# Listing the evictions of out in block order in a fused attention and FFN kernel, with the work of every engine listed anew

## The chip, the cores and the metric

The kernel runs on one core of one Trainium2 chip. The metric is the device time of one execution in microseconds (us); the time of the kernel before is the median of 3 runs. Engines are called as in the profile: PE is TensorE's matrix unit and PEld its weight loads, DVE is VectorE, ACT is ScalarE, POOL is GpSimd, SP is SyncE, which here only issues DMAs.

## The reference

```python
# batch 8, heads 8, seq 576, head_dim 64; d_model 512, d_ff 1024, 4608 tokens
def _attn_ref(q, k, v):
    q_s = np.exp(q - q.max(-1, keepdims=True))
    q_s = q_s / (q_s.sum(-1, keepdims=True) + 1e-09)
    k_s = np.exp(k - k.max(2, keepdims=True))
    k_s = k_s / (k_s.sum(2, keepdims=True) + 1e-09)
    kv = np.einsum('bhsd,bhse->bhde', k_s, v)
    return np.einsum('bhsd,bhde->bhse', q_s, kv)

def _moe_ref(x, w1, w2, w3, w_out):
    a = x @ w1
    b = x @ w2
    h = a * b @ w3
    return h @ w_out
```

The output of the attention, with its heads side by side, is x of 4608 tokens by 512, and the output of the FFN is the result. All inputs and the output are float32.

## The kernel before

**Fold.** Since nothing stands between w3 and w_out, their product W3O = w3 @ w_out (1024 x 512) is made once at the start. w3 is loaded in six parts (`w3.0` to `w3.5`), w_out in two (`wo.0`, `wo.1`); for each of 8 row blocks ft, `w3t.ft` transposes on PE (L444), `w3T.ft` copies the transposed block out of PSUM, `pf.ft.0` and `pf.ft.1` multiply it with the two halves of w_out (L456), and `W3O.ft` evicts the product. Zero matmuls (L351, 17 at the very start and some ahead of one named step) fill time in which PE has nothing to do; the table `FILL` says ahead of which.

**Attention**, for each batch b. Steps are named for what they do, with b and, for most, the part of the tile: `q`, `k`, `v` load; `qmx` (L581) takes the maxima of q, `qsub` (L586) subtracts them, `qexp` is the exponential, `qsm`, `qeps`, `qrc` sum it and take the reciprocal, `qn` (L618) divides. The quotient is transposed on PE (`qt`, evicted by `qT`) or by a transposing DMA on SP's queue (`qd`, L641). `kmx`, `cba`, `cbx`, `cb` (L488 to L519) find the maxima of k, `ksub` (L523) subtracts, `kexp` (L531) is the exponential, `vc` casts v to float16. `kv` (L548, 72 small matmuls, then a few for the sum of k's exponentials) multiplies k and v, `kve` and `kv2` divide. `xm` (L666) and `xt` multiply with q and give x transposed, evicted by `xs` and `xts`.

**FFN**, for each token chunk c. Chunks 0 to 7 hold 512 tokens of batch c each, chunk 8 the remaining 64 tokens of all batches. For each of eight blocks u of d_ff: `up.1.c.sub.u` multiplies with w2 into a PSUM buffer of the ring pab, `bs.c.sub.u` evicts it as float16 to bsb (on ACT or DVE, L324), `up.0.c.sub.u` multiplies with w1 into another buffer of pab (both L783), and `ab.c.sub.u` (DVE, L798) multiplies the two. Then for each block of 128 tokens tb, `down.c.tb` multiplies with W3O into one of the two buffers of po (L805; L820 in chunk 8), `os.c.tb` evicts it to osb (ACT or DVE, L324) and `st.c.tb` stores it. The rings have 4 buffers in pab, 2 in po, 4 in osb, 4 in bsb. Chunks 0 and 1 are cut in two by `sub`, so that they can start before all of x is there.

**The order** is written out by hand: `ORDER` lists all 793 steps, and `Plan.run` (L48) emits them in that order, so each engine executes its own steps in the order of the list. For the flexible steps `PICKS` names the engine. Up to place `LINKED` of the list, steps of DVE and POOL that share a port are also tied to each other in list order. `Plan.run` checks that what a step needs is listed ahead of it, its `after` too; `after` makes no wait on the chip, it only says what has to be listed earlier. The buffers of a ring are those of the tile pool: which one a step gets, and whose release it waits for on the chip, follows from the order in which the list emits takes and releases. Loads listed in `LOADS` are issued on POOL's queue, with at most eight under way; those of `LATE` on SP's, where the stores and the transposing DMAs are too.

The places in the old list that matter below:

```
q.1.0 v.0 w3T.4 pf.5.1 ... kv.0 kve.0 ... qsub.1.0 w3t.1 pf.6.0 w3T.1 kv2.0
down.3.0 down.3.1 bs.4.0.1 qd.5.1 qd.5.0 os.3.1 os.3.0 v.7 down.3.2
```

Of the kernel before, what the change touches and what calls it, by code (L numbers as in the profile page):

```python
# [77 lines left out]
q.0.0 qmx.0.0 q.0.1 qmx.0.1 qsub.0.1 qexp.0.1 w3.4 wo.0 ident wo.1 qsub.0.0 w3.0 k.0 w3.2 w3.3 w3.5  # L78
w3t.4 w3t.5 w3T.5 pf.5.0 qsm.0.1 q.1.0 v.0 w3T.4 pf.5.1 qexp.0.0 qeps.0.1 qrc.0.1 qsm.0.0 w3.1 w3t.0
k.1 qn.0.1 qeps.0.0 pf.4.0 qrc.0.0 pf.4.1 qt.0.16 W3O.5 qn.0.0 w3T.0 qT.0.16 W3O.4 qt.0.8 pf.0.0  # L80
qt.0.0 w3t.2 w3T.2 w2.0 pf.0.1 w3t.3 w3T.3 kmx.0.0 cba.0 W3O.0 qT.0.8 cbx.0 pf.2.0 qT.0.0 pf.2.1
w1.0 w1.1 pf.3.0 w3t.7 w2.1 W3O.2 w3T.7 pf.3.1 w3t.6 pf.7.0 pf.7.1 w1.2 cb.0 ksub.0.1 kexp.0.1
ksub.0.0 kexp.0.0 kv.0 kve.0 w2.2 w3T.6 W3O.3 qmx.1.0 W3O.7 k.2 qsub.1.0 w3t.1 pf.6.0 w3T.1 kv2.0
xm.0.0 xs.0.0.0 xs.0.0.1 pf.1.0 pf.1.1 w2.3 xm.0.1 kmx.1.0 cba.1 pf.6.1 xs.0.1.1 xs.0.1.0 qexp.1.0
w1.3 v.1 q.1.1 q.2 cbx.1 qsm.1.0 up.1.0.0.0 xt.0 bs.0.0.0 up.0.0.0.0 up.1.0.1.0 up.0.0.1.0 ab.0.0.0
cb.1 qeps.1.0 ksub.1.1 ksub.1.0 bs.0.1.0 up.1.0.0.1 bs.0.0.1 ab.0.1.0 up.0.0.0.1 up.1.0.1.1
up.0.0.1.1 ab.0.0.1 bs.0.1.1 up.1.0.0.2 up.0.0.0.2 up.1.0.1.2 ab.0.1.1 up.0.0.1.2 W3O.1 kexp.1.1
qrc.1.0 xts.0.0 bs.0.0.2 up.1.0.0.3 ab.0.0.2 bs.0.1.2 kmx.2.0 kexp.1.0 cba.2 qn.1.0 bs.0.0.3 W3O.6
xts.0.1 up.0.0.0.3 up.1.0.1.3 ab.0.0.3 down.0.0 ab.0.1.2 cbx.2 cb.2 ksub.2.0 bs.0.1.3 kv.1
up.0.0.1.3 qmx.1.1 ksub.2.1 ab.0.1.3 kve.1 os.0.0 qsub.1.1 kv2.1 down.0.1 down.0.2 qd.1.0 kexp.2.0  # L90
kexp.2.1 os.0.1 qmx.2.1 xm.1.0 xs.1.0.1 xs.1.0.0 qmx.2.0 qsub.2.1 down.0.3 qexp.1.1 os.0.2
up.1.1.0.0 qsm.1.1 up.0.1.0.0 up.1.1.0.1 qexp.2.1 qeps.1.1 bs.1.0.0 qsm.2.1 qrc.1.1 qsub.2.0 v.2
vc.2.0 vc.2.1 ab.1.0.0 qexp.2.0 qsm.2.0 qn.1.1 qeps.2.1 bs.1.0.1 up.0.1.0.1 up.1.1.0.2 ab.1.0.1
qrc.2.1 st.0.0 k.3 q.3 kv.2 bs.1.0.2 qeps.2.0 kve.2 up.0.1.0.2 up.1.1.0.3 up.0.1.0.3 os.0.3 kv2.2
qt.1.16 qt.1.8 bs.1.0.3 ab.1.0.2 ab.1.0.3 qrc.2.0 down.1.0 qn.2.1 qT.1.8 qT.1.16 xm.1.1 xs.1.1.0
st.0.1 st.0.2 v.3 down.1.1 qn.2.0 qmx.3.0 qmx.3.1 qsub.3.0 qd.2.1 qd.2.0 kmx.3.0 xs.1.1.1 xt.1
up.1.1.1.0 up.0.1.1.0 xts.1.0 qexp.3.0 xts.1.1 os.1.1 bs.1.1.0 up.1.1.1.1 up.0.1.1.1 ab.1.1.0
bs.1.1.1 xm.2.0 cba.3 up.1.1.1.2 up.0.1.1.2 ab.1.1.1 qsm.3.0 xs.2.0.1 xs.2.0.0 xm.2.1 bs.1.1.2
up.1.1.1.3 up.0.1.1.3 cbx.3 xs.2.1.1 xs.2.1.0 up.1.2.0.0 ab.1.1.2 qsub.3.1 up.0.2.0.0 cb.3 bs.1.1.3
qeps.3.0 qrc.3.0 ab.1.1.3 st.0.3 k.4 qexp.3.1 bs.2.0.0 up.1.2.0.1 up.0.2.0.1 up.1.2.0.2 q.4 v.4 q.5  # L100
os.1.0 ksub.3.1 ksub.3.0 qsm.3.1 down.1.2 down.1.3 vc.3.1 qeps.3.1 vc.3.0 kmx.4.1 qrc.3.1 ab.2.0.0
kmx.4.0 cba.4 kexp.3.1 kexp.3.0 bs.2.0.1 up.0.2.0.2 os.1.3 ab.2.0.1 bs.2.0.2 qn.3.0 qmx.4.1 qn.3.1
ab.2.0.2 os.1.2 cbx.4 cb.4 up.1.2.0.3 kv.3 kve.3 kv2.3 bs.2.0.3 up.0.2.0.3 ab.2.0.3 up.1.2.0.4
up.0.2.0.4 xt.2 qd.3.0 qd.3.1 xts.2.1 up.1.2.0.5 up.0.2.0.5 xts.2.0 vc.4.0 qsub.4.1 bs.2.0.4 qmx.4.0
ab.2.0.4 bs.2.0.5 ab.2.0.5 xm.3.1 xm.3.0 xs.3.1.0 up.1.2.0.6 up.0.2.0.6 up.1.2.0.7 xs.3.0.1 xs.3.0.0
bs.2.0.6 xs.3.1.1 qmx.5.1 ksub.4.0 qsub.4.0 vc.4.1 ab.2.0.6 qexp.4.1 qexp.4.0 up.0.2.0.7 up.1.3.0.0
bs.2.0.7 up.0.3.0.0 up.1.3.0.1 qsm.4.1 ab.2.0.7 qeps.4.1 qsm.4.0 qrc.4.1 qsub.5.1 up.0.3.0.1
ksub.4.1 bs.3.0.0 qn.4.1 kexp.4.0 qeps.4.0 up.1.3.0.2 bs.3.0.1 down.2.0 qexp.5.1 kexp.4.1 ab.3.0.0
st.1.1 qrc.4.0 k.5 st.1.2 kmx.5.1 qmx.5.0 st.1.0 v.5 vc.5.0 st.1.3 q.6 ab.3.0.1 up.0.3.0.2 down.2.1
os.2.0 qd.4.1 qn.4.0 qd.4.0 kv.4 xt.3 bs.3.0.2 qsub.5.0 kmx.5.0 kve.4 os.2.1 cba.5 ab.3.0.2 down.2.2  # L110
down.2.3 vc.5.1 qexp.5.0 os.2.2 up.1.3.0.3 xts.3.1 os.2.3 xts.3.0 kv2.4 xm.4.0 qsm.5.1 bs.3.0.3
qeps.5.1 xm.4.1 xt.4 qsm.5.0 up.0.3.0.3 cbx.5 cb.5 qeps.5.0 xts.4.1 xts.4.0 qmx.6.0 ab.3.0.3
xs.4.0.0 xs.4.0.1 xs.4.1.1 xs.4.1.0 k.6 qrc.5.0 up.1.3.0.4 bs.3.0.4 up.0.3.0.4 up.1.3.0.5 up.0.3.0.5
ab.3.0.4 up.1.3.0.6 up.0.3.0.6 bs.3.0.5 ab.3.0.5 bs.3.0.6 up.1.3.0.7 up.0.3.0.7 up.1.4.0.0 qrc.5.1
ksub.5.1 ksub.5.0 q.7 st.2.2 kmx.6.1 kexp.5.1 kexp.5.0 ab.3.0.6 kv.5 up.0.4.0.0 st.2.1 qsub.6.0
qmx.7.0 qn.5.1 qn.5.0 bs.3.0.7 ab.3.0.7 bs.4.0.0 up.1.4.0.1 kve.5 ab.4.0.0 kmx.6.0 st.2.3 st.2.0 v.6
up.0.4.0.1 down.3.0 down.3.1 bs.4.0.1 qd.5.1 qd.5.0 os.3.1 os.3.0 v.7 down.3.2 qmx.6.1 kv2.5 cba.6
ab.4.0.1 up.1.4.0.2 os.3.2 xm.5.0 xm.5.1 xt.5 bs.4.0.2 cbx.6 qexp.6.0 xts.5.0 xts.5.1 up.0.4.0.2
up.1.4.0.3 up.0.4.0.3 up.1.4.0.4 qsub.7.0 qsub.6.1 vc.6.1 vc.6.0 qmx.7.1 xs.5.0.0 bs.4.0.3 xs.5.1.1
qexp.6.1 ab.4.0.2 qsm.6.0 ab.4.0.3 cb.6 bs.4.0.4 xs.5.1.0 up.0.4.0.4 ab.4.0.4 xs.5.0.1 up.1.4.0.5  # L120
up.0.4.0.5 bs.4.0.5 ab.4.0.5 up.1.4.0.6 up.0.4.0.6 bs.4.0.6 ab.4.0.6 up.1.4.0.7 up.0.4.0.7 bs.4.0.7
up.1.5.0.0 up.0.5.0.0 ksub.6.1 qeps.6.0 kexp.6.1 down.3.3 qsub.7.1 ab.4.0.7 up.1.5.0.1 up.0.5.0.1
ksub.6.0 vc.7.0 kexp.6.0 qexp.7.0 bs.5.0.0 qsm.6.1 qeps.6.1 qrc.6.0 qn.6.0 ab.5.0.0 qrc.6.1 qexp.7.1
bs.5.0.1 st.3.0 k.7 st.3.1 qn.6.1 vc.7.1 qsm.7.0 os.3.3 qsm.7.1 up.1.5.0.2 kv.6 up.0.5.0.2 kve.6
bs.5.0.2 down.4.0 down.4.1 os.4.0 qeps.7.0 down.4.2 up.1.5.0.3 ab.5.0.1 kv2.6 qd.6.0 qd.6.1 st.3.2
xm.6.0 ab.5.0.2 kmx.7.1 os.4.1 os.4.2 xm.6.1 xt.6 bs.5.0.3 st.3.3 qeps.7.1 qrc.7.1 qn.7.1 qd.7.1
st.4.0 up.0.5.0.3 xts.6.0 xts.6.1 ab.5.0.3 xs.6.0.0 xs.6.1.1 xs.6.0.1 kmx.7.0 up.1.5.0.4 up.0.5.0.4
up.1.5.0.5 bs.5.0.4 ab.5.0.4 bs.5.0.5 up.0.5.0.5 up.1.5.0.6 up.0.5.0.6 up.1.5.0.7 cba.7 ab.5.0.5
up.0.5.0.7 xs.6.1.0 cbx.7 bs.5.0.6 cb.7 ksub.7.1 ab.5.0.6 bs.5.0.7 ab.5.0.7 up.1.6.0.0 up.0.6.0.0
down.4.3 bs.6.0.0 ab.6.0.0 up.1.6.0.1 up.0.6.0.1 bs.6.0.1 ab.6.0.1 up.1.6.0.2 up.0.6.0.2 bs.6.0.2  # L130
up.1.6.0.3 up.0.6.0.3 ab.6.0.2 up.1.6.0.4 up.0.6.0.4 os.4.3 down.5.0 bs.6.0.3 up.1.6.0.5 ksub.7.0
qrc.7.0 qn.7.0 kexp.7.0 kexp.7.1 kv.7 ab.6.0.3 os.5.0 kve.7 st.4.1 st.4.2 qd.7.0 st.4.3 bs.6.0.4
ab.6.0.4 down.5.1 down.5.2 os.5.1 bs.6.0.5 kv2.7 os.5.2 up.0.6.0.5 xm.7.0 xm.7.1 xt.7 ab.6.0.5
xs.7.1.0 xts.7.1 xts.7.0 up.1.6.0.6 up.0.6.0.6 xs.7.1.1 bs.6.0.6 xs.7.0.0 xs.7.0.1 ab.6.0.6
up.1.6.0.7 up.0.6.0.7 up.1.7.0.0 up.0.7.0.0 bs.6.0.7 up.1.7.0.1 ab.6.0.7 down.5.3 bs.7.0.1 bs.7.0.0
ab.7.0.0 up.0.7.0.1 up.1.7.0.2 up.0.7.0.2 up.1.7.0.3 ab.7.0.1 up.0.7.0.3 bs.7.0.3 bs.7.0.2 ab.7.0.2
up.1.7.0.4 ab.7.0.3 up.0.7.0.4 up.1.7.0.5 up.0.7.0.5 bs.7.0.4 ab.7.0.4 bs.7.0.5 up.1.7.0.6
up.0.7.0.6 up.1.7.0.7 ab.7.0.5 up.0.7.0.7 bs.7.0.6 bs.7.0.7 ab.7.0.6 up.1.8.0.0 up.0.8.0.0 down.6.0
st.5.0 os.5.3 ab.7.0.7 os.6.0 down.6.1 down.6.2 st.5.1 os.6.1 down.6.3 bs.8.0.0 up.1.8.0.1 ab.8.0.0
up.0.8.0.1 up.1.8.0.2 bs.8.0.1 ab.8.0.1 st.5.2 os.6.2 down.7.0 up.0.8.0.2 up.1.8.0.3 up.0.8.0.3  # L140
st.5.3 st.6.2 bs.8.0.2 ab.8.0.2 os.7.0 st.6.0 st.6.1 os.6.3 down.7.1 os.7.1 st.7.1 st.7.0 bs.8.0.3
st.6.3 ab.8.0.3 up.1.8.0.4 bs.8.0.4 down.7.2 os.7.2 up.0.8.0.4 down.7.3 ab.8.0.4 os.7.3 up.1.8.0.5
bs.8.0.5 up.0.8.0.5 ab.8.0.5 up.1.8.0.6 up.0.8.0.6 bs.8.0.6 ab.8.0.6 up.1.8.0.7 bs.8.0.7 st.7.2
up.0.8.0.7 ab.8.0.7 down.8.0 down.8.1 os.8.0 down.8.2 os.8.1 down.8.3.0 os.8.2 down.8.3 st.7.3
st.8.0 st.8.1 st.8.2 os.8.3.0 st.8.3.0 os.8.3 st.8.3
# [778 lines left out]
```

## Time and profile before

| what | value |
|---|---|
| time, median of 3 runs | 240.86 us (240.09 to 241.2) |
| profiled execution, its own time | 240.74 us |
| span of the profiled execution | 239.0 us |
| PE busy | 229.9 us, 96% of the span |
| DVE busy | 179.8 us, 75% |
| ACT busy | 118.0 us, 49% |
| POOL busy | 111.4 us, 47% |

The profile is of one execution. Its span runs from the first to the last instruction that it shows; the execution's own time is 1.7 us longer. A row of the timeline has start, length, engine, line, operation, output and inputs with their shapes, and in brackets how long the engine had been idle before it and what ended that. A row of the waits has the engine and what it waited for, then the sum, the number of times and the longest.

### The profile page before, as it was taken

Reading aid. Unit: us, or ns where it says so; the run is one execution under the profiler, and the core shown is the slowest. Engines: PE = TensorE matmul, PEld = TensorE weight load, DVE = VectorE, ACT = ScalarE, POOL = GpSimd, SP = SyncE. Lnnn points to the kernel's source line nnn. Section 1 sums busy time; section 2 is a strip of 40 time slices with the busy share of each in tenths; the row PEclk is TensorE's granted clock in tenths of the full one; section 3 lists DMA queues with packets and bytes.
Section 4 is the critical chain, followed back from the end, with each engine's and each line's share of the span. In section 5 each row is a group of like instructions: output and inputs, shape, how many; then the busy total and the mean of one; then the engine's idle time right before and its main releaser. Section 6 shows DMA issues by size and latency. Waiting matters only on the chain.

```text
span 239.0 us, 4936 instructions
## 1 busy us (share of the span) xinstructions
PE 229.9 (96%) x1971; PEld 120.1 (50%) x1971; DVE 179.8 (75%) x273; ACT 118.0 (49%) x222; POOL 111.4 (47%) x74
## 2 busy tenths in 40 slices
...
GB/s 210 217 304 252 295 210 300 245 270 329 393 290 295 397 225 231 381 278 263 346 234 235 310 3 44 145 48 139 0 134 88 4 0 0 44 134 21 199 44 132
DMA packets 38998, 45.93 MB, mean 192 GB/s; under 512 B 17088, under 2 KB 23488, under 8 KB 38976
## 3 DMA queue, kind: packets, MB, share of 16 engines
...
q8 instruction: 15, 0.25, 0.4%
q14 instruction: 7, 0.06, 0.1%
...
## 4 chain that ended last, share of the span: by engine, by line
PE 76%; DMA 13%; POOL 4%; DVE 3%; ACT 1%; issue 1%; POOLq 0%; ACTq 0%
PE pab L783 47%; PE po L805 21%; DMA v<-in_v_dram 7%; DMA wosb<-in_moe_w_out_dram 4%; PE po L820 3%; DMA qT<-en 3%; POOL k L523 2%; PE pkv L548 2%; PE xm L666 1%; DVE kmx L497 1%; POOL q L586 1%; POOL en L618 1%; DVE kmx L498 1%; PE po L666 1%; ACT osb L324 0%
## 5 line engine op out<-in xcount | busy, mean ns | idle before, releaser
L798 DVE TENSOR_TENSOR ab<-pab,bsb 128x512 f16<-128x512 f32 x72 | 48.9, 682 | 25.9 <-PE pab L783 14.5
L783 PE MATMUL pab<-x,w1sb 128*128 128x512 f16 (+1 forms) x320 | 66.0, 337 | 0.0
L783 PE MATMUL pab<-x,w2sb 128*128 128x512 f16 (+1 forms) x320 | 65.9, 337 | 0.0
L805 PE MATMUL po<-W3O,ab 128*128 128x512 f16 x256 | 58.9, 379 | 0.7 <-ACT osb L324 0.7
L783 PEld LDWEIGHTS <-w2sb 128*128 128x128 f16 x352 | 34.0, 98 | 28.3 <-issue 0.9
L783 PEld LDWEIGHTS <-w1sb 128*128 128x128 f16 x352 | 33.7, 98 | 26.7
L324 ACT CAST bsb<-pab 128x512 f16<-128x512 f32 x46 | 26.8, 585 | 35.0 <-PE pab L783 29.0
L523 POOL TENSOR_TENSOR k<-k,cb 128x1152 f32<-128x1152 f32 x13 | 34.0, 2629 | 19.2 <-DVE cb L519 17.0
L805 PEld LDWEIGHTS <-ab 128*128 128x128 f16 x256 | 24.7, 98 | 29.9 <-issue 1.4
L324 ACT COPY osb<-po 128x512 f32<-128x512 f32 (+1 forms) x28 | 16.0, 571 | 41.6 <-PE po L805 31.9
L618 POOL TENSOR_TENSOR en<-eq,qr 128x1280 f16<-128x1280 f16 (+1 forms) x12 | 25.8, 2165 | 12.8 <-DMA out_dram<-osb 6.1
L586 POOL TENSOR_TENSOR q<-q,qm 128x1280 f32<-128x1280 f32 (+1 forms) x13 | 27.8, 2149 | 6.5 <-DMA qT<-en 4.5
L581 DVE TENSOR_REDUCE qm<-q 128x16 f32<-128x1024 f32 (+1 forms) x16 | 21.4, 1341 | 3.7 <-DMA q<-in_q_dram 3.7
L324 DVE CAST bsb<-pab 128x512 f16<-128x512 f32 x26 | 17.7, 685 | 6.2 <-PE pab L783 5.9
L599 DVE TENSOR_REDUCE qr<-eq 128x20 f32<-128x1280 f16 (+1 forms) x16 | 21.4, 1340 | 1.0 <-ACT eq L594 0.7
L531 ACT ACTIVATE ek<-k 128x1152 f16<-128x1152 f32 x16 | 18.3, 1161 | 5.3 <-POOL k L523 4.9
L594 ACT ACTIVATE eq<-q 128x1280 f16<-128x1280 f32 (+1 forms) x16 | 18.3, 1160 | 2.1 <-DVE q L586 1.7
L488 DVE TENSOR_REDUCE km<-k 128x128 f32<-128x1152 f32 x8 | 17.1, 2132 | 0.0
L456 PE MATMUL po<-wosb,w3T 128*128 128x512 f16 x64 | 15.6, 379 | 1.4 <-DMA wosb<-in_moe_w_out_dram 1.3
L324 DVE COPY osb<-po 128x512 f32<-128x512 f32 x9 | 6.2, 687 | 7.4 <-PE po L805 7.4
L328 ACT ACTIVATE x<-xm 128x512 f16<-128x512 f32 x16 | 9.1, 596 | 4.6 <-PE xm L666 4.5
L456 PEld LDWEIGHTS <-w3T 128*128 128x128 f16 x64 | 5.7, 98 | 7.6 <-issue 1.8
...
## 6 DMA issues: line engine op xcount, KB each, us to landing
...
```

The costliest lines, as they stand in the source:

```text
L324: return [(nc.scalar.copy if eng == "ACT" else engine[eng].tensor_copy)(out=out, in_=in_)]
L456: nc.tensor.matmul(st["pf", ft], lhsT=st["w3T", ft][:, gt, :], rhs=wosb[:, gt, :], start=(gt == 0), stop=(gt == N_FT - 1))
L523: return [engine[eng].tensor_tensor(out=kb[:, two(hp), :, :], in0=kb[:, two(hp), :, :], in1=st["cb", b][:, two(hp), None, :].broadcast_to( ...
L531: nc.scalar.activation(out=st["ek", b][:, hp, :, :].rearrange("p j (i d) -> p i j d", i=2), in_=kb[:, two(hp), :, :], func=AF.Exp)
L581: dve.tensor_reduce(out=st["qm", b][:, :, j], in_=qb[:, :, j, :], axis=AX.X, op=ALU.max)
L586: return [engine[eng].tensor_tensor(out=qb[:, :, j, :], in0=qb[:, :, j, :], in1=st["qm", b][:, :, j, None].broadcast_to([P, HH, n, D]), op ...
L594: nc.scalar.activation(out=st["eq", b, p], in_=qb[:, :, j, :], func=AF.Exp)
L599: dve.tensor_reduce(out=st["qr", b][:, :, slice(*PARTS[p])], in_=st["eq", b, p], axis=AX.X, op=ALU.add)
L618: return [engine[eng].tensor_tensor(out=st["en", b][:, j, :, :].rearrange("p j h d -> p h j d"), in0=st["eq", b, p], in1=st["qr", b][:, :, ...
L783: nc.tensor.matmul(st["p", one, c, sub, u][:, a * (t1 - t0):(a + 1) * (t1 - t0)], lhsT=w[:, ct, fb * P:(fb + 1) * P], rhs=x()[:, ct, t0:t1 ...
L798: dve.tensor_tensor(out=st["ab", c][:, nf * u:nf * u + nf, t0:t1], in0=cut(st["p", 0, c, sub, u]), in1=cut(st["bsb", c, sub, u]), op=ALU.mult)
L805: nc.tensor.matmul(st["po", c, tb], lhsT=st["ab", c][:, ft, tb * P:(tb + 1) * P], rhs=W3O[:, ft, :], start=(ft == 0), stop=(ft == N_FT - 1))
```

## The change

Each `os` step gets the previous one of its chunk (for the first, the last of the chunk before) in its `after`, so that the evictions of out have to be listed strictly in the order of their blocks. `ORDER`, `PICKS`, `LOADS` and `LATE` are written anew under that rule. The six zero matmuls stand ahead of `pf.4.0` instead of `pf.5.0`. The steps are the same 793, and what PE computes is the same.

```diff
 FILL = {
-    "begin": 17, "pf.5.0": 6,
+    "begin": 17, "pf.4.0": 6,
 }
...
+        old_os = [("os", c - 1, 3)] if c else []
...
                     A(("os", c, tb), moves(C), 0, lambda eng, tb=tb: os(tb, eng), [("down", c, tb)],
-                      lead=EVICT, gives=[("down", c, tb)], takes="osb")
+                      lead=EVICT, gives=[("down", c, tb)], takes="osb", after=old_os)
+                    old_os = [("os", c, tb)]
...
-                      lead=EVICT, gives=[("down", *it)], takes="osb")
+                      lead=EVICT, gives=[("down", *it)], takes="osb", after=old_os)
+                    old_os = [("os", *it)]
```

The loads:

```diff
 LOADS = [
-    ("w3", 4), ("wo", 0), ("wo", 1), ("w3", 0), ("k", 0), ("w3", 2), ("w3", 3), ("w3", 5), ("q",
-    1, 0), ("v", 0), ("w3", 1), ("k", 1), ("w2", 0), ("w1", 0), ("w1", 1), ("w2", 1), ("w1", 2),
-    ("w2", 2), ("k", 2), ("w2", 3), ("w1", 3), ("v", 1), ("q", 1, 1),
+    ("w3", 4), ("wo", 0), ("w3", 0), ("wo", 1), ("k", 0), ("w3", 2), ("w3", 3), ("w3", 5),
+    ("w3", 1), ("v", 0), ("q", 1, 0), ("k", 1), ("w2", 0), ("w1", 0), ("w2", 1), ("w1", 1),
+    ("w1", 2), ("w2", 2), ("k", 2), ("w2", 3), ("w1", 3), ("v", 1), ("q", 1, 1),
 ]
...
 LATE = [
-    ("q", 2), ("v", 2), ("k", 3), ("q", 3), ("v", 3), ("k", 4), ("q", 4), ("v", 4), ("q", 5),
-    ("k", 5), ("v", 5), ("q", 6), ("k", 6), ("q", 7), ("v", 6), ("v", 7), ("k", 7),
+    ("q", 2), ("v", 2), ("k", 3), ("q", 3), ("v", 3), ("k", 4), ("v", 4), ("q", 4), ("q", 5),
+    ("v", 5), ("k", 5), ("v", 6), ("q", 6), ("k", 6), ("v", 7), ("q", 7), ("k", 7),
 ]
```

And from the new list, the places that answer to those shown above, and those that the prediction speaks of:

```
qT.0.8 w3t.1 ksub.0.1 kexp.0.0 W3O.7 w3T.6 ... kv.0 k.2 kve.0 kv2.0 pf.6.0 pf.6.1 ... qmx.1.0 qsub.1.0
...
vc.3.1 qrc.3.1 down.1.2 qn.3.1 kmx.4.0 cba.4 qmx.4.1 up.0.2.0.3 kexp.3.0 kv.3 ... kv2.3 ab.2.0.2
...
down.3.0 os.3.0 down.3.1 down.3.2 qd.5.1 st.3.0 q.7 k.7 cbx.6 bs.4.0.0 ab.4.0.0 os.3.1 os.3.2
...
up.1.7.0.5 bs.7.0.5 bs.7.0.4 ab.7.0.3 up.0.7.0.5
...
bs.8.0.4 bs.8.0.3 ab.8.0.2 ab.8.0.3 up.0.8.0.4
```

Of the flexible steps, `PICKS` puts 7 fewer on DVE (73 instead of 80) and 7 more on ACT (148 instead of 141); POOL has 45 in both. Among them `qsub.1.0` goes from POOL to DVE, 8 of the `bs` from DVE to ACT, and two of the `os` from ACT to DVE.

More of the change, by code (lines that the diff above doesn't have):

```diff
@@ L77 @@
 ORDER = """
[L78 to L145, printed above, removed]
+q.0.0 qmx.0.0 qsub.0.0 q.0.1 qmx.0.1 w3.4 ident wo.0 qexp.0.0 qsm.0.0 qsub.0.1 w3.0 wo.1 w3t.4 k.0
+w3.2 w3.3 qeps.0.0 qrc.0.0 w3t.5 w3T.4 pf.4.0 w3t.0 w3.5 w3.1 w3T.5 qn.0.0 v.0 q.1.0 pf.5.0 qexp.0.1
@@ new lines @@
+qt.0.0 pf.4.1 pf.5.1 qT.0.0 W3O.4 qsm.0.1 qeps.0.1 qrc.0.1 qn.0.1 qt.0.16 qt.0.8 k.1 w3T.0 pf.0.0
+w3t.2 pf.0.1 kmx.0.0 qT.0.16 cba.0 W3O.5 w3t.3 w3T.2 pf.2.0 pf.2.1 W3O.0 w3T.3 cbx.0 W3O.2 pf.3.0
+w3t.7 w2.0 w1.0 w3t.6 pf.3.1 w3T.7 cb.0 ksub.0.0 pf.7.0 pf.7.1 w2.1 w1.1 qT.0.8 w3t.1 ksub.0.1
+kexp.0.0 W3O.7 w3T.6 w3T.1 kexp.0.1 W3O.3 w1.2 w2.2 kv.0 k.2 kve.0 kv2.0 pf.6.0 pf.6.1 w2.3 xm.0.0
+qmx.1.0 qsub.1.0 pf.1.0 pf.1.1 xs.0.0.0 xs.0.0.1 xm.0.1 xs.0.1.0 xs.0.1.1 up.1.0.0.0 bs.0.0.0
+qexp.1.0 up.0.0.0.0 xt.0 up.1.0.1.0 w1.3 kmx.1.0 cba.1 cbx.1 ab.0.0.0 v.1 cb.1 q.1.1 ksub.1.0
@@ new lines @@
+ksub.1.1 bs.0.1.0 up.0.0.1.0 up.1.0.0.1 ab.0.1.0 up.0.0.0.1 up.1.0.1.1 up.0.0.1.1 bs.0.0.1
+up.1.0.0.2 bs.0.1.1 qsm.1.0 ab.0.0.1 up.0.0.0.2 ab.0.1.1 xts.0.1 W3O.1 qeps.1.0 W3O.6 bs.0.0.2
+qrc.1.0 up.1.0.1.2 bs.0.1.2 up.0.0.1.2 ab.0.0.2 up.1.0.0.3 q.2 kmx.2.0 ab.0.1.2 up.0.0.0.3 cba.2
+kexp.1.0 xts.0.0 kexp.1.1 bs.0.0.3 cbx.2 ab.0.0.3 cb.2 qn.1.0 ksub.2.0 kexp.2.0 up.1.0.1.3
+up.0.0.1.3 ksub.2.1 qmx.1.1 down.0.0 kv.1 os.0.0 bs.0.1.3 ab.0.1.3 down.0.1 down.0.2 qd.1.0 kve.1
+qsub.1.1 kv2.1 os.0.1 os.0.2 xm.1.0 qmx.2.1 xs.1.0.0 down.0.3 xs.1.0.1 qmx.2.0 qsub.2.1 qexp.1.1
@@ new lines @@
+qsm.1.1 up.1.1.0.0 up.0.1.0.0 up.1.1.0.1 up.0.1.0.1 bs.1.0.0 up.1.1.0.2 kexp.2.1 qsub.2.0 v.2
+qexp.2.1 vc.2.0 qeps.1.1 vc.2.1 ab.1.0.0 qexp.2.0 qrc.1.1 qsm.2.1 qsm.2.0 qn.1.1 bs.1.0.1 ab.1.0.1
+bs.1.0.2 qeps.2.1 kv.2 kve.2 qrc.2.1 up.0.1.0.2 up.1.1.0.3 up.0.1.0.3 qeps.2.0 os.0.3 kv2.2 qn.2.1
+st.0.0 k.3 q.3 v.3 st.0.3 st.0.1 qt.1.8 qt.1.16 qd.2.1 ab.1.0.2 bs.1.0.3 qrc.2.0 ab.1.0.3 down.1.0
+qmx.3.0 qT.1.8 qT.1.16 xm.1.1 xs.1.1.1 xs.1.1.0 qmx.3.1 down.1.1 qn.2.0 qsub.3.0 kmx.3.0 qd.2.0 xt.1
+qsub.3.1 xts.1.0 qexp.3.0 up.1.1.1.0 up.0.1.1.0 vc.3.0 bs.1.1.0 up.1.1.1.1 up.0.1.1.1 xts.1.1 os.1.0
@@ new lines @@
+bs.1.1.1 xm.2.0 ab.1.1.0 cba.3 up.1.1.1.2 up.0.1.1.2 xs.2.0.1 k.4 xs.2.0.0 xm.2.1 ab.1.1.1 qsm.3.0
+cbx.3 xs.2.1.0 cb.3 xs.2.1.1 qeps.3.0 bs.1.1.2 ab.1.1.2 up.1.1.1.3 bs.1.1.3 up.0.1.1.3 ab.1.1.3
+up.1.2.0.0 up.0.2.0.0 up.1.2.0.1 up.0.2.0.1 qrc.3.0 qexp.3.1 ksub.3.1 bs.2.0.0 kmx.4.1 v.4
+up.1.2.0.2 ab.2.0.0 up.0.2.0.2 bs.2.0.1 up.1.2.0.3 q.4 qsm.3.1 kexp.3.1 os.1.1 ab.2.0.1 qn.3.0
+ksub.3.0 qeps.3.1 bs.2.0.2 vc.3.1 qrc.3.1 down.1.2 qn.3.1 kmx.4.0 cba.4 qmx.4.1 up.0.2.0.3 kexp.3.0
+kv.3 kve.3 vc.4.1 st.0.2 q.5 qd.3.0 up.1.2.0.4 cbx.4 bs.2.0.3 os.1.2 st.1.0 qd.3.1 kv2.3 ab.2.0.2
```

55 lines of the change are left out of this document (49 added, 6 removed), and 94 rows, old and new, of the table PICKS.

## The prediction

> **What bounds the kernel now.** I read the page's busy times first, then what TensorE waited for, then stretches of 20 us, then the timeline around each wait.
>
> ```profile
> span 239.0 us, 4936 instructions
> PE 229.9 (96%) x1971; PEld 120.1 (50%) x1971; DVE 179.8 (75%) x273; ACT 118.0 (49%) x222; POOL 111.4 (47%) x74
> ```
>
> TensorE (PE) is busy 229.9 us of 239.0; the next engine, VectorE (DVE), 179.8. What can be gained is PE's idle time, 9.1 us, and its waits have names:
>
> ```profile
> PE po L351 <- DVE zero L346: 1.5, 1, 1.5
> PE po L456 <- DMA wosb<-in_moe_w_out_dram: 1.3, 1, 1.3
> PE w3t L444 <- DMA w<-in_moe_w_dram: 1.0, 2, 0.8
> PE pkv L548 <- DMA v<-in_v_dram: 0.9, 1, 0.9
> PE po L805 <- ACT osb L324: 0.7, 1, 0.7
> PE xm L666 <- DMA qT<-en: 0.5, 1, 0.5
> ```
>
> They sum to 5.9; the other 3 us are the end, after the last matmul. The first three lie before 20 us, the fourth ends at 28.15, the sixth at 55.75, the fifth at 128.30. Where none lies, PE has no gap:
>
> ```profile
> 120.00:140.00 20.00, 19.32 (x171) 8.87 (x170) 17.66 (x27) 8.75 (x20) 15.22 (x9) 1.00 0.73 230
> 180.00:200.00 20.00, 20.00 (x107) 9.03 (x106) 11.21 (x20) 4.78 (x9) 0.00 (x0) 1.00 0.12 27
> 200.00:220.00 20.00, 20.00 (x95) 9.06 (x93) 8.57 (x14) 2.25 (x4) 0.00 (x0) 1.00 0.23 53
> 220.00:239.00 19.00, 15.88 (x82) 7.77 (x80) 4.70 (x7) 4.85 (x9) 0.00 (x0) 1.00 0.45 124
> ```
>
> The columns are length, then busy time of PE, weight loads, DVE, ScalarE (ACT), GpSimd (POOL), granted clock, DMA share, GB/s. The clock is 1.00 throughout. So one microsecond of engine work moved from DVE to ACT is worth nothing by itself; only a wait of PE that goes or comes counts. The sum is made against the profiled execution (240.74 us: a span of 239.0 and 1.7 around it), 0.12 under the median of the runs, 240.86.
>
> **The rule itself.** The added `after=old_os` asks that the evictions of out be listed in block order; it adds no wait on the chip. But the listing hands out the buffers: an accumulator taken by a later step is the one whose eviction is listed earliest among those still free. In the old list `os.3.1` (ACT) stands ahead of `os.3.0` (DVE), so `down.3.2` takes the buffer of `down.3.1`, the product directly before it:
>
> ```profile
> 124.01 3.62 PE L805 MATMUL po<-W3O,ab 128*128 128x512 f16 x16
> 125.94 0.69 DVE L324 COPY osb<-po 128x512 f32<-128x512 f32 x1 [0.63 <-PE po L805]
> 127.66 0.59 ACT L324 COPY osb<-po 128x512 f32<-128x512 f32 x1 [3.73 <-PE po L805]
> 128.30 1.89 PE L805 MATMUL po<-W3O,ab 128*128 128x512 f16 x8 [0.68 <-ACT osb L324]
> ```
>
> `os.3.0` had freed the other buffer at 126.63, a microsecond before PE was done with `down.3.1` at 127.64, yet PE stood 0.68 until `os.3.1` ended. In the new list `os.3.0` is ahead, `down.3.2` takes the buffer free since long: **−0.68**. Nothing behind it was timed by this wait: the windows after it are full, so it is the whole amount.
>
> **The same trap elsewhere.** The rule covers `os`, not `bs`, the evictions of the w2 product. Among these the new list has two pairs out of order: `bs.7.0.5` (ACT) ahead of `bs.7.0.4` (DVE), and `bs.8.0.4` (ACT) ahead of `bs.8.0.3` (DVE). By the same handing out, `up.0.7.0.5` takes the buffer that `up.1.7.0.5` has just filled, and `up.0.8.0.4` that of `up.1.8.0.4`; each must wait until ACT has emptied it, with no matmul between. No `up` of the old list waits for the `up` directly before it. Before, this stretch ran so:
>
> ```profile
> 195.98 1.03 PE L783 MATMUL pab<-x,w2sb 128*128 128x512 f16 x4
> 196.84 1.03 PE L783 MATMUL pab<-x,w1sb 128*128 128x512 f16 x4
> 197.04 0.69 DVE L324 CAST bsb<-pab 128x512 f16<-128x512 f32 x1
> 198.81 0.59 ACT L324 CAST bsb<-pab 128x512 f16<-128x512 f32 x1 [2.91 <-PE pab L783]
> ```
>
> PE went straight on while the eviction ran. The price of the new wait is that of the old one: an ACT eviction of 128x512 takes 0.59 in both forms, and at 128 PE lost 0.68 to it (0.02 to start, 0.59, some 0.06 to PE). ACT is free there (busy 4.78 and 2.25 us of 20 in the two windows), so it starts at once: two times 0.68, **+1.36**. Bounds: 0 if the wait were hidden, up to 0.9 each if ACT is at another eviction for a third of one. Behind PE's wait only the multiplies `ab` are queued on DVE, which is idle half of that time; nothing is made up later, since PE has no gap to shrink from there to the end.
>
> **The start.** PE's order ahead of `kv.0` changes: the eight transposes of `w3t.1` come before it instead of after.
>
> ```profile
> 28.15 0.77 PE L548 MATMUL pkv<-v,ek 64*64 64x64 f16 x72 [0.90 <-DMA v<-in_v_dram]
> 29.39 0.71 PE L444 MATMUL w3t<-ident,w 128*128 128x128 f16 x8
> 29.94 1.03 PE L456 MATMUL po<-wosb,w3T 128*128 128x512 f16 x4
> 25.48 2.43 ACT L531 ACTIVATE ek<-k 128x1152 f16<-128x1152 f32 x2 [0.21 <-DVE k L523]
> ```
>
> The transposes take 29.39 to 29.94, 0.55 us, and fall into the 0.90 that PE waits for v.0: **−0.55**. `kv.0` itself hardly moves: v.0 is now requested behind w3.1 instead of q.1.0, and may land sooner or later by a little, but the exponentials of k end at 27.91, and their chain (k.0, the tree of maxima on DVE) is as it was, so at most −0.13 and I take 0. On the other side wo.1 is now requested after w3.0. The wait of 1.3 for it may grow, but `w3t.0` and `pf.5.0` are moved ahead of it; PE has 0.90−0.55 = 0.35 in hand before `kv.0`, so a growth beyond that costs. The first `up` of w1 waits for a w1.0 requested behind as much data as before; I allow +0.1. The six zero matmuls go from `pf.5.0` to `pf.4.0`: in PE's order they stand after the same transposes of `w3t.5`, so 0. The seven steps fewer on DVE and seven more on ACT (some 0.6 us each) lie beside PE everywhere: 0.
>
> **The wait at 55.** `xm.1.0` waits for a transposing DMA whose source is made on POOL:
>
> ```profile
> 30.62 1.92 POOL L586 TENSOR_TENSOR q<-q,qm 128x1024 f32<-128x1024 f32 x1
> 32.58 1.23 DVE L497 TENSOR_TENSOR kmx<-k 128x1024 f32<-128x1024 f32 x1 [0.55 <-POOL q L586]
> 39.22 5.20 POOL L523 TENSOR_TENSOR k<-k,cb 128x1152 f32<-128x1152 f32 x2 [2.10 <-DVE cb L519]
> 47.47 1.91 POOL L618 TENSOR_TENSOR en<-eq,qr 128x1024 f16<-128x1024 f16 x1 [3.05 <-ACT xtail L328]
> 49.41 6.21 DMA qT<-en
> 55.75 0.41 PE L666 MATMUL xm<-qT,kv 64*64 64x256 f16 x8 [0.48 <-DMA qT<-en]
> qT<-en SPq DMA_TRANSPOSE x13, 3.5
> ```
>
> POOL and DVE are linked in list order here: `kmx.2.0` follows `ksub.1`, `qn.1.0` follows `kmx.2.0`. The new list does `qsub.1.0` on DVE (1.24 by the row of a tree step of the same 1024 columns, instead of 1.92 on POOL), and the tree of k.1 starts sooner. By the rows `ksub.1` then begins some 1.1 sooner, at 38.1, and `qn.1.0` ends at 48.4 instead of 49.38. With the same 6.2 the DMA, issued at 48.45, lands at 54.65; PE was there at 55.27 (55.75−0.48) and, 0.45 ahead by the start, comes at 54.82: the whole wait goes, **−0.48**, and PE's lead there becomes 0.55−0.10+0.48 = 0.93. Bounds of the DMA: 3.5 (the median of 13) changes nothing more; at 7.1 it lands at 55.55, and all of this and 0.25 of the start's gain is lost.
>
> **`kv.2`.** Here PE gives some back. POOL does `qsub.2.1`, `qsub.2.0`, `vc.2.0` in a row; they start when the maxima of q.2 are there, which takes 1.49 from its landing (issued at 45.6, landed 9.1 later; timeline, and above it the tile view of that one load):
>
> ```profile
> L405 SPq DMA_DIRECT2D q<-in_q_dram x1: 367/367/367, 45.6 to 45.6; - x1
> DMA to landing us min/median/max: 9.1/9.1/9.1
> 54.71 1.49 DVE L581 TENSOR_REDUCE qm<-q 128x20 f32<-128x1280 f32 x1
> 54.13 6.53 POOL L586 TENSOR_TENSOR q<-q,qm 128x1280 f32<-128x1280 f32 x3
> 60.58 1.16 POOL L324 CAST v<-v 128x1152 f16<-128x1152 f32 x1
> 62.29 0.78 PE L548 MATMUL pkv<-v,ek 64*64 64x65 f16 x72
> ```
>
> That chain ends at 61.74 before and is fed by a load, not by PE: 61.6 after, where PE would come at 62.29−0.93 = 61.36. **+0.24**, bounds 0 to +0.4.
>
> **Sum.** −0.55 +0.10 −0.48 +0.24 −0.68 +1.36 = −0.01. From 60 to 127 I walked the new order against the rows; the shortest distances between a product's data and PE are 0.1 to 0.4 us, so I add +0.1 for one that fails: 240.8 for the profiled execution, **240.9** for the median.
>
> **Rivals.**
>
> 1. Faster: the two waits do not come. For: at 128 alone one is seen, and for `bs` none. Against: it is the same ring and engine. Then 240.9−1.36 = 239.5.
>
> 2. The start's gain is lost in the DMA queue. For: the transposing DMA took 6.2 where the median is 3.5, while q.2 (45.6 to 54.7) was still in flight; issued sooner it meets more of that load. Then +0.48, and a start 0.55 poorer at worst: 241.4 to 241.9. The Trainium skill, "DMA: Bandwidth & Descriptors", section "Issuing engines are not separate DMA queues", says that transfers started from different engines run on the same DMA engines and interleave; that speaks for this rival, and by it the sum would be 241.4 with the 55 us wait kept.
>
> 3. Slower: DVE's queue is blocked near 86. The new list puts `qmx.4.1` ahead of `kv2.3` and `ab.2.0.2`, and requests q.4 after v.4.
>
> ```profile
> L405 SPq DMA_DIRECT2D v<-in_v_dram x1: 497/497/497, 73.5 to 73.5; - x1
> DMA to landing us min/median/max: 12.5/12.5/12.5
> 87.34 1.48 DVE L581 TENSOR_REDUCE qm<-q 128x20 f32<-128x1280 f32 x1
> ```
>
> The v.4 request, last of three, landed 12.5 us later at 86.0, and q.4 now takes that place. DVE ran `qmx.4.1` at 87.34; with one multiply fewer ahead of it (0.6) it reaches it at 86.7. From then on each microsecond that q.4 is late is one of PE's, since `ab.2.0.2` behind it frees the pab buffers. Landing at 86.0 costs nothing, at 88.0 it makes 240.9+1.3 = 242.2; later, more.
>
> 4. The change doesn't do what it says: the rule only reorders a list, and everything else stays. Then only the 0.68 goes: 240.2.
>
> **Chances and range.** A difference of 0.5% (1.2 us) is about what a measurement of this kernel can tell from none: faster is below 239.66, slower above 242.06. The forecast 0.58 and rival 4 0.04 are within; rival 2, 0.12, too; rival 1 0.13, of which most is faster; rival 3 0.13, slower. Of the forecast's own share 0.05 crosses the upper line (POOL chains at 60 to 110). That makes 0.12 faster, 0.70 same, 0.18 slower. The range is 239.7 to 242.2: the bounds of the costs above reach 1.2 down (waits hidden) and 1.3 up (start lost, one middle stall, or the beginning of rival 3).
>
> **What would show it.** In PE's waits two entries of pab on ACT's bsb near 195 and 214, 0.6 to 0.7 each, and no wait of po on osb: right. None of pab: rival 1. A wait of `xm` on qT that stays near 0.5: rival 2. DVE idle before an L581 reduction between 85 and 89, and PE idle just after: rival 3. The forecast is wrong if PE's idle between 60 and 190 exceeds 0.5, or if its idle in all differs from 9.1 by over 1.2.

## The result and the profile after

The changed kernel takes 242.13 us in the median of 6 runs (242.07 to 242.47), the kernel before 240.87 (6 runs, 240.09 to 241.2). The ratio is 1.0059 with a 95% interval of 1.0045 to 1.0073: slower by 1.26 us, where 240.9, no change, had been forecast. The profiled execution took 242.10 us, with a span of 240.3.

The page of the changed kernel, its span, its busy times and its loads of instructions; and of the kernel before, the last of these lines, which the prediction does not show (queue, packets, MB, share of the DMA engines):

```profile
span 240.3 us, 4941 instructions
PE 229.3 (95%) x1971; PEld 119.6 (50%) x1971; DVE 173.5 (72%) x266; ACT 122.6 (51%) x229; POOL 112.8 (47%) x74
q14 instruction: 8, 0.07, 0.1%
```

```profile
q14 instruction: 7, 0.06, 0.1%
```

DVE has lost 6.3 us of work and ACT has gained 4.6, and the time has risen: the share of busy time says nothing here. What TensorE waited for in the changed kernel:

```profile
PE w3t L445 <- DMA w<-in_moe_w_dram: 3.1, 2, 2.3
PE po L352 <- DVE zero L347: 1.6, 1, 1.6
PE pab L784 <- ACT bsb L325: 1.3, 2, 0.7
PE po L457 <- DMA wosb<-in_moe_w_out_dram: 0.4, 1, 0.4
PE pab L784 <- DMA w1sb<-in_moe_w_dram: 0.3, 1, 0.3
```

The wait of po on osb is gone, and so are those for v.0 and for qT; two waits of pab on bsb have come, 1.3 us in all. These are the entries that the prediction had named. The waits in the first 20 us have grown from 3.8 to 5.1, but 1.2 of that only takes the place of work: the 17 zero matmuls ahead took 5.20 in this execution and 6.43 in that of before, and the first transposes start at 9.04 instead of 8.75. `kv.0` starts at 28.00 instead of 28.15, straight behind the transposes of `w3t.1`, with no wait for k or v left.

The two new waits, in the timeline of PE and ACT of the changed kernel:

```profile
194.76 1.03 PE L784 MATMUL pab<-x,w2sb 128*128 128x512 f16 x4
195.83 0.58 ACT L325 CAST bsb<-pab 128x512 f16<-128x512 f32 x1 [2.87 <-PE pab L784]
196.46 1.02 PE L784 MATMUL pab<-x,w1sb 128*128 128x512 f16 x4 [0.67 <-ACT bsb L325]
...
214.59 1.03 PE L784 MATMUL pab<-xtail,w2sb 128*128 128x512 f16 x4
215.65 0.58 ACT L325 CAST bsb<-pab 128x512 f16<-128x512 f32 x1 [11.01 <-PE pab L784]
216.29 1.02 PE L784 MATMUL pab<-xtail,w1sb 128*128 128x512 f16 x4 [0.67 <-ACT bsb L325]
```

The brackets say 0.67. From start to start a product of four matmuls takes 0.86 where PE runs on (195.98 to 196.84 in the rows shown of before); here it takes 196.46 − 194.76 = 1.70. So a wait for the product just made costs 0.84, not 0.67. The other 0.17 is what a product's row (1.03) exceeds the distance (0.86): where PE runs on, the next product starts 0.17 before the row of the last one ends, and here it can't. (The profile models the ends of matmuls; the 0.84 rests on starts alone.)

The rest of the loss lies after the last matmul. The last eviction of the changed kernel starts at 236.37, that of the kernel before at 235.96 (timeline of ACT):

```profile
236.37 0.37 ACT L325 COPY osb<-po 128x256 f32<-128x256 f32 x1 [0.46 <-PE po L821]
```

```profile
235.96 0.37 ACT L324 COPY osb<-po 128x256 f32<-128x256 f32 x1 [0.55 <-PE po L820]
```

Behind the last store SP waits for it to land. From 230 on, SP's wait for that in the changed kernel, then in the kernel before:

```profile
SPq L923 <- DMA out_dram<-osb: 1.7, 1, 1.7
```

```profile
SPq L919 <- DMA out_dram<-osb: 0.8, 1, 0.8
```

PE and ACT are 0.41 later than before at the last eviction; the other 0.94 of the 1.35 us that the span has grown is the wait for the last store. In that stretch, from 238 to 239, the changed kernel's DMAs are these (kind of queue, packets, MB, share):

```profile
q1 hardware_dynamic: 25, 0.02, 5.5%
q14 instruction: 1, 0.01, 2.0%
```

A load of 8 KB of instructions starts at 238.22, while the last store is being written. 15 of the 16 parts of that store have signalled by 238.46, the last one at 239.41. No packet of the store starts between 238.11 and 238.53, which is when the 0.31 us of the load are over; its last nine packets follow one by one until 238.95, so they stood behind the load on one DMA engine. In the trace of before no such load lies in the span's end; the next one comes at 240.01, when all is done.

To see what each place of the list was worth, every step of PE in one trace was matched with the same step of the other, and the differences of the time from its start to the next start were summed up. PE stands, against the kernel before and on the same work (minus is ahead):

| up to | predicted | measured |
|---|---|---|
| start of `kv.0` (28 us) | −0.55 | −0.70 |
| end of the first `up.0` (36) | −0.45 | −0.23 |
| `xm.1.0` (55) | −0.93 | −0.60 |
| `kv.2` (62) | −0.69 | −0.6 |
| 120 us | −0.6 | −0.7 |
| `down.3.2` (125) | −1.3 | −1.5 |
| ahead of 194 | −1.3 | −1.2 |
| after 217 | +0.1 | +0.45 |
| end of the span | +0.1 | +1.35 |

### The profile page after: what moved, and what is told of

The parts are those of the page before. It is cut to its first block, busy times and chain, and to the rows that moved or that the text cites. A ratio compares the mean times of both kernels' runs of the same rounds, so it can differ in the third digit from the quotient of the medians.

```text
span 240.3 us, 4941 instructions
## 1 busy us (share of the span) xinstructions
PE 229.3 (95%) x1971; PEld 119.6 (50%) x1971; DVE 173.5 (72%) x266; ACT 122.6 (51%) x229; POOL 112.8 (47%) x74
## 4 chain that ended last, share of the span: by engine, by line
PE 83%; DMA 12%; POOL 1%; issue 1%; ACT 1%; POOLq 0%
PE pab L784 52%; PE po L806 23%; DMA w1sb<-in_moe_w_dram 6%; DMA w<-in_moe_w_dram 6%; PE po L821 3%; PE pkv L549 2%; PE xm L667 1%; PE po L667 1%; ACT bsb L325 0%; POOL wosb L406 0%; POOL k L406 0%; POOL w L406 0%; PE qtp L634 0%; PE xt L667 0%; PE pkv L559 0%
## 5 line engine op out<-in xcount | busy, mean ns | idle before, releaser
L325 ACT CAST bsb<-pab 128x512 f16<-128x512 f32 x54 | 31.1, 585 | 49.8 <-PE pab L784 49.7
L619 POOL TENSOR_TENSOR en<-eq,qr 128x1024 f16<-128x1024 f16 (+1 forms) x15 | 31.5, 2107 | 8.5 <-DVE qr L612 4.6
L587 POOL TENSOR_TENSOR q<-q,qm 128x1280 f32<-128x1280 f32 (+1 forms) x12 | 25.8, 2161 | 9.1 <-DMA qT<-en 4.4
L325 ACT COPY osb<-po 128x512 f32<-128x512 f32 (+1 forms) x26 | 14.8, 569 | 26.8 <-PE po L806 22.0
L600 DVE TENSOR_REDUCE qr<-eq 128x16 f32<-128x1024 f16 (+1 forms) x16 | 21.4, 1337 | 0.5 <-ACT eq L595 0.4
L595 ACT ACTIVATE eq<-q 128x1024 f16<-128x1024 f32 (+1 forms) x16 | 18.7, 1168 | 2.6 <-DVE q L587 1.8
L325 DVE COPY osb<-po 128x512 f32<-128x512 f32 x11 | 7.5, 685 | 15.0 <-PE po L806 9.3
L325 DVE CAST bsb<-pab 128x512 f16<-128x512 f32 x18 | 12.3, 682 | 7.0 <-PE pab L784 6.5
L329 ACT ACTIVATE x<-xm 128x512 f16<-128x512 f32 x18 | 10.3, 599 | 4.1 <-PE xm L667 4.1
```

The costliest lines, as they stand in the source:

```text
L325: return [(nc.scalar.copy if eng == "ACT" else engine[eng].tensor_copy)(out=out, in_=in_)]
L587: return [engine[eng].tensor_tensor(out=qb[:, :, j, :], in0=qb[:, :, j, :], in1=st["qm", b][:, :, j, None].broadcast_to([P, HH, n, D]), op ...
L595: nc.scalar.activation(out=st["eq", b, p], in_=qb[:, :, j, :], func=AF.Exp)
L600: dve.tensor_reduce(out=st["qr", b][:, :, slice(*PARTS[p])], in_=st["eq", b, p], axis=AX.X, op=ALU.add)
L619: return [engine[eng].tensor_tensor(out=st["en", b][:, j, :, :].rearrange("p j h d -> p h j d"), in0=st["eq", b, p], in1=st["qr", b][:, :, ...
```

## The experiments

Each kernel was timed in 5 rounds beside the kernel before, whose median in these sessions lay between 240.72 and 240.86; the ratios go by the runs of the same session.

**The two waits of pab.** Both pairs in block order, then only the first:

```diff
-up.1.7.0.5 bs.7.0.5 bs.7.0.4 ab.7.0.3 up.0.7.0.5
+up.1.7.0.5 bs.7.0.4 bs.7.0.5 ab.7.0.3 up.0.7.0.5
...
-st.5.3 st.5.2 os.6.2 bs.8.0.4 bs.8.0.3
+st.5.3 st.5.2 os.6.2 bs.8.0.3 bs.8.0.4
```

> The changed kernel with two pairs of evictions listed in block order: bs.7.0.4 ahead of bs.7.0.5, bs.8.0.3 ahead of bs.8.0.4. Theory: the two pab waits of TensorE are 0.84 us of its time each (from start to start, 1.70 instead of 0.86), so both go and the time falls by 1.7 to about 240.4. Rival: the wait only stands in place of another one that follows at once (the ab product, or the stores), and the time falls by less than 0.8, to 241.4 or more.

240.39 us, ratio 0.9981 (0.9967 to 0.9995): 1.74 less than the changed kernel. The waits of pab on bsb are gone from the list of waits, and nothing stands in their place.

> The changed kernel with only bs.7.0.4 and bs.7.0.5 in block order. Theory: each of the two pab waits stands for itself, 0.84 us: 241.3, with the wait at 214 left. Rival: the second wait grows when the first is gone (TensorE comes sooner to the same eviction): 241.8 or more.

241.31 us, ratio 1.0027 (1.0014 to 1.0041): 0.82 less than the changed kernel, and one wait of 0.7 is left. Each wait stands for itself, and 2 x 0.84 is what they cost: step for step against the changed kernel's trace, that of `bs_order` gains 0.84 at each of the two places. The rival falls.

**The wait of po, alone.** The kernel before with one pair turned round:

```diff
-down.3.0 down.3.1 bs.4.0.1 qd.5.1 qd.5.0 os.3.1 os.3.0 v.7 down.3.2
+down.3.0 down.3.1 bs.4.0.1 qd.5.1 qd.5.0 os.3.0 os.3.1 v.7 down.3.2
```

> The kernel before with os.3.0 listed ahead of os.3.1 and nothing else. Theory: the po wait at 128 goes, 0.84 us from start to start: 240.0. Rival: TensorE then waits for something else behind it: 240.5 or more.

240.05 us, ratio 0.9960 (0.9943 to 0.9978). The 0.84 that was expected is within the interval (0.5 to 1.4), and the entry of po on osb is gone.

**The load of instructions at the end.** Copies of one column from a tile to itself, that nothing reads, ahead of all other work; 12 on ACT in the changed kernel, 4 on ACT in the kernel before, 12 on DVE in the changed kernel:

```diff
+    idle = konst.tile([P, 2], F32, name="idle")
+    dve.memset(idle, 0.0)
+    for _ in range(12):
+        nc.scalar.copy(out=idle[:, 1:2], in_=idle[:, 0:1])
```

> The changed kernel with 12 one-column copies more on ScalarE at the very start, where it waits for its first data. Theory: the last store lands 0.95 us late because an 8 KB load of instructions at 238.2 us takes one of the 16 DMA engines, and that load is ScalarE's; 12 instructions more make it come earlier, away from the last store: span's end 1.8 us after the last ScalarE copy instead of 3.6, time about 241.2. Rival: the late landing is not tied to ScalarE's instructions (the store's own spread, another engine's load): 242.1, and the load of instructions stays at 238.2.

241.31 us, ratio 1.0019 (1.0006 to 1.0031), 0.8 less than the changed kernel. The load that stood at 238.22 now starts at 231.12. From the start of the last ACT copy to the end of the span it is 239.7 − 236.70 = 3.0 us, as in the kernel before, where the changed kernel has 3.9 (the lengths in the expectation, 1.8 and 3.6, were wrong, and so was their difference; the 0.95 was right). It is not the start that gained: by the matched steps PE is 0.33 behind the changed kernel at the last matmul. The last eviction of this kernel, SP's wait for the last store, and the load among the DMAs between 231 and 232:

```profile
236.70 0.37 ACT L325 COPY osb<-po 128x256 f32<-128x256 f32 x1 [0.46 <-PE po L826]
```

```profile
SPq L928 <- DMA out_dram<-osb: 0.8, 1, 0.8
```

```profile
q14 instruction: 1, 0.01, 1.9%
```

> The kernel before with 4 one-column copies more on ScalarE at the very start; it then has as many ScalarE instructions as the changed kernel. Theory: the load of instructions that came at 240.0, after the end, comes into the last store; the time rises by 0.9 to about 241.8, with nothing else changed. Rival: 240.9.

241.50 us, ratio 1.0027 (1.0014 to 1.0040): 0.74 above the kernel before, a little less than expected. The load came from 240.0 to 237.41, so that it lies between 237 and 238, and the wait for the last store has grown; SP's wait, and the load among the DMAs of that stretch:

```profile
SPq L924 <- DMA out_dram<-osb: 1.5, 1, 1.5
```

```profile
q14 instruction: 1, 0.01, 3.7%
```

Four copies that do nothing, at a time when ACT has nothing to do, cost 0.7 us at the other end of the kernel.

> A control: the changed kernel with 12 one-column copies more on VectorE instead of ScalarE. Theory: the load of instructions in the end is ScalarE's, so it stays near 238.2 and the time at 242.1. Rival: instructions of any engine move it, or the 12 copies do good in the start: 241.3, as with the copies on ScalarE.

242.03 us, ratio 1.0055 (1.0041 to 1.0070): as the changed kernel. The load starts at 237.84. SP's wait for the last store in this kernel, and the load among the DMAs between 237.5 and 238.5:

```profile
SPq L928 <- DMA out_dram<-osb: 1.3, 1, 1.3
```

```profile
q14 instruction: 1, 0.01, 3.5%
```

So it is ACT's own instructions that decide when this load comes, and the theory stands in all three. What the 12 copies on DVE moved is another load of queue 14, from 185.8 to 170.7, which the 12 on ACT left at 186.4.

**The start.** The changed kernel with `w3t.1` behind `kv.0` again:

```diff
-qT.0.8 w3t.1 ksub.0.1 kexp.0.0 W3O.7 w3T.6 w3T.1 kexp.0.1
+qT.0.8 ksub.0.1 kexp.0.0 W3O.7 w3T.6 kexp.0.1
...
-kv.0 k.2 kve.0 kv2.0 pf.6.0 pf.6.1 w2.3 xm.0.0
+kv.0 k.2 kve.0 w3t.1 pf.6.0 w3T.1 kv2.0 pf.6.1 w2.3 xm.0.0
```

> The changed kernel with the transposes of w3t.1 (and their eviction) behind kv.0 again, as in the kernel before. By the prediction's step they save 0.55 ahead of kv.0, so this kernel takes 242.65. Theory now: TensorE comes to the first w1 product ahead of w1.0, which lands at 34.9, so the wait there (0.30) gives back what is lost, and only 0.2 to 0.3 is left: 242.4.

242.22 us, ratio 1.0064 (1.0049 to 1.0080): 0.1 above the changed kernel. The intervals alone don't tell that from 0.5; the traces show where it goes. The timeline of PE of this kernel:

```profile
27.99 0.77 PE L549 MATMUL pkv<-v,ek 64*64 64x64 f16 x72 [0.56 <-ACT ek L532]
...
34.12 1.05 PE L784 MATMUL pab<-x,w2sb 128*128 128x256 f16 x8
35.01 1.04 PE L784 MATMUL pab<-x,w1sb 128*128 128x256 f16 x8
```

and of the changed kernel:

```profile
33.61 1.05 PE L784 MATMUL pab<-x,w2sb 128*128 128x256 f16 x8
34.95 1.05 PE L784 MATMUL pab<-x,w1sb 128*128 128x256 f16 x8 [0.30 <-DMA w1sb<-in_moe_w_dram]
```

The lead of half a microsecond is there at 33.6 and all but gone at 35: w1.0 lands at 34.8 to 34.9 in both, and in the changed kernel PE waits for it. At the last matmul this kernel is 0.3 behind the changed one all the same, lost at 46 to 52 us; but other kernels with no edit there differ from the changed one by 0.15 to 0.36 at 45, so this is not shown to be the price of `w3t.1`. It doesn't appear in the time because SP's wait for the last store is 1.4 here instead of 1.7.

**The transposing DMA at 55.** First the changed kernel with `qsub.1.0` on POOL:

```diff
-    "qsub_1_0": "DVE",
+    "qsub_1_0": "POOL",
```

> The changed kernel with qsub.1.0 on GpSimd again, as in the kernel before. By the prediction's step the transposing DMA is issued about 1 us later and TensorE waits for it near 54: 0.5 us more, 242.6. Rival: the DMA is held by the loads beside it and not by the time of its issue, or VectorE's freed time makes up for it: 242.1.

243.62 us, ratio 1.0122 (1.0105 to 1.0140): 1.5 above the changed kernel, more than either had said, and by another way. Between 30 and 60, PE's waits have this entry:

```profile
PE pab L784 <- DVE ab L799: 1.8, 2, 0.9
```

DVE's timeline shows the step that is late, and the tile view of the transposing DMA how long it took:

```profile
35.16 1.23 DVE L498 TENSOR_TENSOR kmx<-k 128x1024 f32<-128x1024 f32 x1 [3.70 <-POOL q L587]
```

```profile
DMA to landing us min/median/max: 3.3/3.3/3.3
```

POOL gets to `qsub.1.0` late, after loads whose issue waits for earlier ones; DVE, tied to it in list order, stands 3.7 us, the multiplies `ab` behind come late, and PE waits twice for pab. The DMA is issued at 50.8 and lands at 54.1, with no wait of `xm` at all: issued 1.9 later than in the changed kernel it landed 0.4 sooner, so the issue does not set the landing. In the changed kernel it was issued at 48.87 and took 5.55, before at 49.41 and took 6.20, and PE came to `xm.1.0` at 55.15. Either alone, the 0.54 of the issue (a landing at 55.07) or the 0.65 of the transfer (54.96), would have taken the wait away; which of them did is not shown.

Two edits of the kernel before were to show what holds it: the store `st.0.0` behind the load k.3, and `os.0.0` on DVE, which holds SP back.

```diff
-qrc.2.1 st.0.0 k.3 q.3 kv.2
+qrc.2.1 k.3 st.0.0 q.3 kv.2
```

```diff
-    "os_0_0": "ACT",
+    "os_0_0": "DVE",
```

> The kernel before with the first store, st.0.0, listed behind the load k.3 instead of ahead of it, so that it is issued near 55.5 instead of 51.8. Theory: the transposing DMA of batch 1 (issued 49.4, landed 55.6) is held by this store beside it, and not by the time of its own issue; it lands near 54.2 and TensorE's wait of 0.48 at 55 goes: 240.3. Rival: it lands 6 us after its issue as before, the wait stays: 240.8.

240.68 us, ratio 1.0005 (0.9993 to 1.0016). The wait of 0.5 is still there, and the DMA takes 6.3. The expectation was wrong about the issue too: k.3 is issued at 51.5 and the store at 52.1, so something stood behind the DMA at the same time as before.

> The kernel before with one entry of the engine table changed: os.0.0 on VectorE, as in the changed kernel, instead of ScalarE. The store st.0.0, and with it everything behind it on SP's queue, is then issued near 53 instead of 51.8. Theory: the transposing DMA of batch 1 (issued 49.4) is slowed by whatever SP issues between 51.5 and 52.2, be it this store or the load k.3; with neither it lands near 54.5 and TensorE's wait at 55 goes or falls under 0.2: 240.35. Rival: what is issued behind it plays no part, it lands 6.2 after its issue and the wait of 0.48 stays: 240.8.

241.01 us, ratio 1.0013 (1.0000 to 1.0025). SP now issues nothing between 51.6 and 54.2, and the DMA still takes 6.3 and lands at 55.8. The theory falls (the load v.2, issued 1.4 to 1.5 behind the DMA in all these traces, was not held back in any). The wait of `xm` is hidden only because PE has a new one ahead of it; PE's waits in this kernel:

```profile
PE po L805 <- DVE osb L324: 0.5, 1, 0.5
```

> The kernel before with two places of the list changed: os.3.0 ahead of os.3.1, and st.0.0 behind k.3. Theory: the two waits lie apart, 240.05 less 0.5: 239.55, without any of the rest of the change. Rival: the gain at 55 is given back at kv.2 (61) or later: 240.0.

240.18 us, ratio 0.9969 (0.9954 to 0.9985), the gain of `os.3.0` alone; the wait at 55 stays.

**Both repairs together**, the pairs of `bs` in order and 12 copies more on ACT:

> Both: the two pairs of evictions in block order and 12 one-column copies more on ScalarE at the start. Theory: the two effects lie in different places (195 and 214, and the end), so they add up: 240.4 less 0.85 to 0.95, about 239.5, faster than both kernels. Rival: with the pab waits gone the last store is late for another reason too, or the two overlap: 240.0 or more.

239.75 us, ratio 0.9958 (0.9944 to 0.9972). The two effects nearly add up (240.39 − 0.8 = 239.6), and the list that lost 0.6% now gains 0.4%. The kernel before with `os.3.0` in order (0.9960) is as fast, by the one edit.

## Why the prediction was wrong

Step by step of the prediction:

- **The rule itself**, `os` in order: right in place and sign. The term was −0.68 and should have been −0.84, by the matched steps and in line with the one edit alone.
- **The same trap elsewhere**, the two pairs of `bs`: right, at 195 and 214 and on ACT, as forecast. Again each was mis-sized, 0.68 for 0.84. With three such waits, one going and two coming, that is +0.16. What the prediction took for the price was PE's idle time in the bracket; the distance from start to start has the lost overlap of 0.17 in it as well.
- **The start**: `w3t.1` did fall into the wait for v.0. The step that failed is "I allow +0.1" for w1.0. PE came earlier to a load that lands at 34.9 whenever PE comes, and lost 0.47 of its 0.70 there (a smaller delay near 45, of which the waits show nothing, took 0.17 more: at 53 no lead was left).
- **The wait at 55** went, as forecast, but the reason was half right: `ksub.1` began 0.95 sooner (38.27), much as forecast, but `qn.1.0` ended only 0.54 sooner (48.84), not 0.98, and the landing is not a fixed time after the issue. That the two together were enough is in part luck. Why the DMA takes 6.2 to 6.5 us in the kernel before and all its variants, and 3.3 to 5.9 in the changed one and its variants, is still open: neither the store st.0.0 nor the load k.3 decides.
- **`kv.2`**: +0.24 was forecast, and nothing came. q.2 landed 7.6 after its issue in the changed kernel, not 9.1, so the chain on POOL ended before PE was there. It took 7.6 in four of the six traces of the old list and its variants too, so 9.1 was one execution's value and no price to build on.
- **60 to 190**: 0.1 was allowed; apart from the 0.84 of `os`, PE lost 0.2 there, with no wait in the list.
- **The end**: the step that decided. The prediction's sum stops at the last matmul and takes the 3 us after it as they were, and it puts the seven steps more on ACT at 0, because they "lie beside PE everywhere". The 3 us grew by 0.94, since ACT's code became longer (4 instructions by the trace, 322 for 318) and its next load of 8 KB fell onto the last store: steps beside PE cost no work of PE, but they move this load. Four copies more on ACT do the same to the kernel before. Without it the time would have been about 241.3: the kernel with 12 copies more on ACT has just that.

So the mechanisms named in the list of work were found, and their sum was off by about 0.35; 0.9 came from a term that the sum had at nothing. That the time lies just inside the stated range is luck: the range's upper end was made up of other losses. **Rival 1**, that the two waits do not come, is out. **Rival 2** came true in its first half: the start's gain was lost to a DMA, but to the load w1.0 and not to the transposing one, whose wait went instead of staying. That is 0.4 us, and not the bulk of the loss. **Rival 3** did not happen: the load of q.4 and DVE's step that needs it, in the changed kernel (tile view of the one load, then the timeline of DVE),

```profile
L406 SPq DMA_DIRECT2D q<-in_q_dram x1: 497/497/497, 71.8 to 71.8; - x1
...
DMA to landing us min/median/max: 11.0/11.0/11.0
```

```profile
86.56 1.48 DVE L582 TENSOR_REDUCE qm<-q 128x20 f32<-128x1280 f32 x1
```

show it landing at 82.8, 3.8 us before DVE is there. **Rival 4** is half true: the rule made its own 0.84, and the new list that came with it gave this and more away.
